# A fifth sequence unit in seven block products, a new order of the first tiles, shifted due times in the planner, and vector sums moved in the last quarter

## The chip, the cores and the metric

The kernel runs on one core of a Trainium2 chip. The metric is the device time of one execution in microseconds (us). Five engines work in parallel, each through its own instructions in its own order: TensorE (PE in the profile; its weight loads are listed as PEld), VectorE (DVE), ScalarE (ACT), GpSimd (POOL) and SyncE (SP), which here only issues DMAs. An instruction waits until what it reads has been written, and until what it overwrites has been read.

## The reference

Two sublayers on 2048 rows of 448 values, in fp32:

```
h  = x + Re(DFT_seq(DFT_hid(layernorm(x))))
     a = xn @ Wd_re^T ; b = xn @ Wd_im^T
     y = Ws_re @ a - Ws_im @ b
h2 = h + (gelu(hn @ w_gate) * (hn @ w_up)) @ w_down      with hn = layernorm(h)
```

w_gate and w_up are 448x1792, w_down is 1792x448. The two sequence matrices are 2048x2048.

## The kernel before

**Precision.** Every fp32 operand is split into two f16 parts, a high one (`hi_part`, a copy on ScalarE, line 105) and a low one, the remainder (`lo_part`, on VectorE, lines 109 and 111). Each product takes three matmuls (high by high, low by high, high by low).

**Stage 1, both transforms.** x stands in 16 tiles of 128 rows. A slot `F i` makes the hidden transform of tile i: 22 matmuls of 448 columns (`feature_mm`, line 456) into two PSUM banks. Two tiles make a unit u (0 to 7). The sequence transform runs in 8 passes p; each pass makes 256 output rows, and in it a slot `U p u` multiplies one unit's features with one block of the sequence matrix (`seq_mm`, line 573). There are two forms of it. A plain unit takes 24 matmuls of 448 columns. An S unit writes the 2x2 block product as seven products (Strassen's scheme): 42 matmuls of 224 columns. It needs sums of the blocks on both sides: of the features, once (`feature_sums`, `sums_high`, `sums_low`, lines 493 to 505), and of the weights, in each pass (`seq_sums`, lines 517 to 521, then `seq_high_s` and `seq_low_s` into the tile `wss`). Before, units 4 to 7 are S units and 0 to 3 are plain (`S_UNITS`, `is_s`). The `F` slots are mixed with the slots of pass 0. Rings: `wr` (raw weights by DMA) has 3 buffers, `ws` (their split) 4, `wss` 2, `wsum` 1.

In the same stretch VectorE and ScalarE also prepare gate and up weights for stage 2 (`Weights`, tiles `gu_s` and `gu_p`), mix finished passes into h (`seq_out`), and take its norm.

**The order in stage 1.** The first three slots (F0, F1, F2) and what they need are written out by hand, from the first load to the last `feature_mm(2, ...)`. Everything after is ordered by a planner: `Task` objects with an engine, a cost, a due time and predecessors. `arranged()` steps through model time; whenever an engine is free it gives it the able task with the earliest due time. The result is only an order of instructions for each engine; on the chip they run when their inputs are there. The slots themselves have a fixed order.

**Stage 2, gate, up, down.** A loop of 56 steps t (four quarters q of 14). In each step PE makes three accumulations X, Y, Z (`GateUp`, matmuls in line 1187), and from t = 14 on the 21 matmuls of one chunk of the down product (`dn_mm`, line 1132). In a step with q of 1 or more, each engine gets its part of this in this order:

- `prev.c_last`: ScalarE's gelu of `c`, then GpSimd's product `hh` (lines 1262, 1264)
- `x_close`; `z_open`, which writes bank Z again and so waits until the step before has read it (`c`, below)
- `dn_split(d+1)`: the next chunk's split, two copies on ScalarE and two low parts on VectorE (line 109)
- 8 matmuls of `dn_mm`; `y_mid`: matmuls into Y, a copy `u` on ScalarE, and on VectorE `hh <- Z, u` (line 1197), which reads Z
- `dn_ahead`: sums for a later chunk, two on GpSimd, one on VectorE (lines 1278 to 1280)
- `do(t, 6)`: in the last quarter the same three sums, all on VectorE, for chunks of the last two row blocks: in t = 44, 46, ... 54, and in 45 and 51
- 10 matmuls of `dn_mm`; `x_open` of the next step
- `y_close` (VectorE reads Y, line 1254); `z_close`: matmuls into Z, which wait until `hh <- Z, u` has read it, then VectorE's `c <- Z, u` (line 1197)
- the last 3 matmuls of `dn_mm`, `y_open`, and `do(t, 7)`: in the step after each of the extra sums their split, `dn_split`, again two copies on ScalarE and two low parts on VectorE.

Of the kernel before, what the change touches and what calls it, by code (L numbers as in the profile page):

```python
# [1 line left out]

# [11 lines left out]
P = 128  # L14
# [18 lines left out]
def kernel(  # L33
# [287 lines left out]
    S_UNITS, WR_BUFS, WS_BUFS, WSS_BUFS, STAGE_BUFS = (4, 5, 6, 7), 3, 4, 2, 2  # L321
# [146 lines left out]
    def is_s(u):  # L468
        return u in S_UNITS
# [30 lines left out]
    def sums_high(i):  # L500
        t = bop[i] = dft.tile([P, 2, 7, HD], F16, name=f"b{i}")
        hi_part(t[:, 0], b32[i][:, 1:8])

    def sums_low(i):
        lo_part(bop[i][:, 1], b32[i][:, 1:8], bop[i][:, 0])
# [57 lines left out]
    def seq_mm(p, u, first, last):  # L563
# [4 lines left out]
        for cc in range(2):  # L568
# [7 lines left out]
            if is_s(u):  # L576
# [132 lines left out]
    plain = [u for u in ORDER if not is_s(u)]  # L709
# [6 lines left out]
    for p in range(1, N_PASS):  # L716
        slots += [("U", p, u) for u in mixed if ("U", p, u) not in early]
# [12 lines left out]
    class Task:  # L730
        def __init__(self, engine, cost, due, what, after=(), begin=0.0, lag=0.15):
            self.engine, self.cost, self.due, self.what = engine, cost, due, what
            self.after, self.begin, self.lag = [t for t in after if t], begin, lag
            self.end = None

    FIRST = 3
    COST = {"F": 4.16, "P": 4.54, "S": 4.02}
    spans = [COST["F" if s[0] == "F" else "S" if is_s(s[2]) else "P"] for s in slots]
# [7 lines left out]
    def chain(engine, costs, due, make, after=()):  # L746

        run, last = [], list(after)

        def step(first):  # L750
            if first:
                run.append(make())
            next(run[0])

        for k, cost in enumerate(costs):
            last = [add(engine, cost, due, lambda k=k: step(k == 0), after=last)]
        return last[0]
# [4 lines left out]
    def fixed(n, rank, engine, cost, what, after=(), lag=0.0):  # L762
        if n < FIRST:
            plan(n, rank, what)
            return None
        return add(engine, cost, T[n + 1], what, after=after, begin=T[n] - 1.0, lag=lag)
# [3 lines left out]
    for k, (i, i2) in enumerate(tiles_of):  # L770
        n = where["F", i]
        if k > 2:
            t = fixed(n - 10, 8, "SP", 0.1, lambda u=i // 2: x_load(u), lag=5.0)
            t = fixed(n - 7, 7, "V", 1.35, lambda i=i, j=i2: x_stats(i, j), [t])
            t = fixed(n - 6, 2, "A", 0.3, lambda i=i, j=i2: x_root(i, j), [t])
            if n - 6 < FIRST:
                fixed(n - 6, 5, "V", 0.6, lambda i=i, j=i2: x_rstd(i, j))
            else:
                t = chain("V", (0.2, 0.1, 0.1, 0.1), T[n - 5], lambda i=i, j=i2: x_rstd_steps(i, j), [t])
            t = fixed(n - 6, 5, "V", 0.15, lambda i=i, j=i2: x_bias(i, j), [t])  # L780
        for c in (i, i2):
            n = where["F", c]
            if k > 2:
                low = fixed(n - 5, 5, "A", 1.15, lambda i=c: x_norm(i), [t])
                low = fixed(n - 5, 5, "V", 0.85, lambda i=c: x_lo(i), [low])
            if k >= 2:
                turned[c] = fixed(n - 4, 2, "SP", 0.1, lambda i=c: x_turn(i), [low] if k > 2 else (), lag=5.0)
                steps[n].after += [t for t in [turned[c]] if t]
        for c in (i, i2):
            n = where["F", c]  # L790
            if not k:
                continue
            done = [steps[n]] if n in steps else []
            if is_s(c // 2):
                t = drained = add("A", 1.05, T[n + 1] + 1.5, lambda i=c: feature_high(i), after=done + ring_w[-2:][:1] * (len(ring_w) > 1))
                t = chain("V", (0.56, 0.36, 0.36), T[n + 2], lambda i=c: feature_sums(i, V), [t])
                t = add("A", 1.45, T[n + 2] + 2.0, lambda i=c: sums_high(i), after=[t])
                t = add("V", 1.7, T[n + 2] + 3.5, lambda i=c: sums_low(i), after=[t])
                ring_w.append(t)
            else:  # L800
                t = add("A", 0.95, T[n + 1] + 1.0, lambda i=c: feature_high(i), after=done)
                t = drained = add("V", 1.07, T[n + 1] + 2.5, lambda i=c: feature_low(i), after=[t])
            bop_of[c] = t
            out_of[n] = drained
    for n, s in enumerate(slots):
        if n < FIRST:
            continue
        if s[0] == "F":
            past = [m for m in out_of if m < n]
            steps[n].after += [out_of[m] for m in sorted(past)[:-1]]  # L810
        elif s[1] == 0:
            steps[n].after += [bop_of[c] for c in (2 * s[2], 2 * s[2] + 1) if c in bop_of]
# [3 lines left out]
    for g, (p, u) in enumerate(units):  # L816
# [5 lines left out]
        else:  # L822
            load = add("SP", 0.1, T[n] - 12.0, lambda p=p, u=u: seq_load(p, u), after=done_with[g - WR_BUFS], lag=5.5)
        if not g:
            done_with[g] = []
            continue
        room = [steps[where["U", *units[g - WS_BUFS]]]] if g >= WS_BUFS else []
        size = 0.9 if is_s(u) else 1.0
        high = add("A", size, T[n] - 1.6, lambda p=p, u=u: seq_high(p, u), after=[load] + room)
        low = add("V", 1.02 if is_s(u) else 1.16, T[n] - 0.4, lambda p=p, u=u: seq_low(p, u), after=[high])  # L830
        done_with[g] = [low]
        if is_s(u):
            t = chain("V", (0.6, 0.34, 0.34), T[n] - 3.0, lambda p=p, u=u: seq_sums(p, u), [load] + sums_of)
            room = [steps[s_units[-WSS_BUFS]]] if len(s_units) >= WSS_BUFS else []
            high_s = add("A", 0.98, T[n] - 1.5, lambda p=p, u=u: seq_high_s(p, u), after=[t, high] + room)
            low_s = add("V", 1.16, T[n] - 0.3, lambda p=p, u=u: seq_low_s(p, u), after=[high_s])
# [8 lines left out]
    for p in range(N_PASS):  # L845
# [3 lines left out]
        load = fixed(n - 6 if p < 2 else n0 - 5, 9, "SP", 0.1, lambda p=p: h_tile(p), h_done.get(p - 4, ()), lag=6.0)  # L849
        if p >= 2:  # L850
            seed = add("A", 1.0, T[n0] - 1.0, lambda p=p: seq_seed(p), after=[load] + rooms[p - 2], begin=T[n0 - 3])
# [4 lines left out]
        copy = add("A", 0.35, t0 + 1.0, lambda p=p: seq_copy(p), after=[steps[n - 1], load] + last_e)  # L856
        mixed_in = chain("V", (1.4 if p < 2 else 0.32, 0.64, 0.86, 0.56), t0 + 5.0, lambda p=p: seq_out(p), [copy])
        rooms[p] = [mixed_in]
        store = add("SP", 0.1, t0 + 6.0, lambda p=p: h_store(p), after=[mixed_in], lag=6.0)
        m = [add("A", 1.75, t0 + 9.0 + 4 * g, lambda q=q, j=j, g=g, p=p: ffn_moments(q, j, hp[q, j], g, junk_of(e_of[p])), after=[mixed_in]) for g in range(2)]  # L860
        t = add("A", 0.25, t0 + 14.0, lambda q=q, j=j: ffn_root(q, j), after=m)
        t = chain("V", (0.2, 0.1, 0.1, 0.1), t0 + 15.0, lambda q=q, j=j: ffn_rstd_steps(q, j), [t])
        last_e, h_done[p] = m, [store, t]
        if q < 2:
            t = add("V", 0.15, t0 + 16.0, lambda q=q, j=j: ffn_bias(q, j), after=[t])
            t = add("A", 1.35, t0 + 17.0, lambda q=q, j=j: ffn_norm_act(q, j, hp[q, j]), after=[t])
            h_done[p] = [store, t]
            for k in range(4):
                t = add("V", 0.36, t0 + 18.0 + k, lambda q=q, j=j, k=k: ffn_sums(q, j, (k,)), after=[t])
            for k in range(2):  # L870
                high = add("A", (0.65, 1.0)[k], t0 + 22.0 + k, lambda q=q, j=j, k=k: ffn_hi(q, j, (k,)), after=[t])
                t = high
            for k in range(5):
                t = add("V", (0.34, 0.87, 0.25, 0.35, 0.25)[k], t0 + 23.0 + k, lambda q=q, j=j, k=k: ffn_lo(q, j, (k,)), after=[t])
            last_e = [t]
            for k in range(4):
                add("SP", 0.1, t0 + 28.0 + k, lambda q=q, j=j, k=k: ffn_transpose(q, j, (k,)), after=[t])
# [17 lines left out]
    begin0 = 12.0  # L895
    raw, freed, stages = None, [], []
    for k, f in enumerate(order):
        gap = (at_end - 10.0 - begin0) / N_DFT
        t0 = begin0 + gap * k
        due = lambda part: t0 + gap * part  # L900
        s1 = add("V", 0.83, due(0.2), lambda f=f: gu[f].sums(True, False), after=[raw] + freed, begin=t0 - 10.0)
        s2 = add("V", 0.95, due(0.3), lambda f=f: gu[f].sums(False, True), after=[s1])
        t, lows = s2, []
        for m in range(4):
            room = stages[-STAGE_BUFS : len(stages) - STAGE_BUFS + 1]
            high = add("A", (0.55, 0.35, 0.55, 0.55)[m], due(0.35 + 0.2 * m), lambda f=f, m=m: gu[f].high(m), after=[t] + room)
            low = add("V", (0.6, 0.34, 0.6, 0.6)[m], due(0.4 + 0.2 * m), lambda f=f, m=m: gu[f].low(m), after=[high])
            stages.append(add("N", 0.0, 0.0, lambda: None, after=[low], lag=7.0))
# [3 lines left out]
        if k + 1 < N_DFT:  # L912
            raw = add("SP", 0.1, due(0.8), lambda f=order[k + 1]: gu_begin(f), after=lows[:2] + [s2], lag=6.5)

    for f in range(2):
        fixed(len(slots) - 6 + 2 * f, 9, "SP", 0.1, lambda f=f: gw_first(f))
    t = fixed(len(slots) - 14, 9, "SP", 0.1, lambda: down_load(0), last_e, lag=6.0)
# [685 lines left out]
```

## Time and profile before

| | us |
|---|---|
| median of 3 runs (712.10 to 712.65) | 712.17 |
| the profiled execution's own time | 712.42 |
| its span, first to last instruction | 710.6 |
| PE busy | 701.3 (99%) |
| DVE busy | 544.6 (77%) |
| ACT busy | 399.8 (56%) |
| POOL busy | 197.1 (28%) |

The granted clock of PE is 1.000 over the span. Times in the rows of the trace count from the first instruction; 1.8 us of the execution's own time lie outside the span. Stage 1 goes to 354.3 us on PE, stage 2 from there to the end. A busy PE is not a PE at its peak; what counts is where its idle time stands and how long a slot lasts.

### The profile page before, as it was taken

The numbers are of one execution on the slowest core, as the hardware profiler recorded it, in microseconds if no ns is written. First come the engines' busy times: TensorE is split into PE (matmuls) and PEld (weight loads), VectorE is DVE, ScalarE is ACT, GpSimd is POOL, SyncE is SP. The second block draws the span as 40 slices with busy tenths as digits, with TensorE's granted clock in tenths as the row PEclk, the third lists the DMA queues.
The fourth block names the chain that finished last, engine by engine and source line by source line (L and its number), as shares of the span: only waits on it lengthen the run. The fifth ranks groups of instructions, "written<-read, shape, count | busy, mean of one in ns | idle before, by whom it ended". The sixth has DMA issues, their size and how long they took to land.

```text
span 710.6 us, 15025 instructions
## 1 busy us (share of the span) xinstructions
PE 701.3 (99%) x5902; PEld 570.6 (80%) x5902; DVE 544.6 (77%) x1131; ACT 399.8 (56%) x845; POOL 197.1 (28%) x225
## 2 busy tenths in 40 slices
PE   7999999999999999999999999999999999999998
PEld 4556567777776868686888889999999999998898
DVE  6799999899988987877368667575765755887876
ACT  5587574757656665645166665555555544454432
POOL 0000000000000000002026664474664745656442
PEclk9999999999999999999999999999999999999999
DMA  9366846799988697758267745847468574445301
GB/s 330 102 151 177 209 155 200 250 206 328 245 221 284 191 245 252 258 162 318 92 238 300 271 172 171 187 165 201 176 196 188 178 208 162 176 156 178 134 28 53
DMA packets 82935, 140.64 MB, mean 198 GB/s; under 512 B 41776, under 2 KB 60464, under 8 KB 82864
## 3 DMA queue, kind: packets, MB, share of 16 engines
q1 hardware_dynamic: 82864, 139.68, 63.8%
q8 instruction: 46, 0.75, 0.4%
q14 instruction: 25, 0.20, 0.1%
HBM read 110.17 MB, written 20.19 MB: 183 GB/s over the span
## 4 chain that ended last, share of the span: by engine, by line
PE 92%; DVE 3%; ACT 2%; issue 1%; DMA 1%; SPq 0%; DVEq 0%; ACTq 0%
PE acc L573 39%; PE acc_d L1132 15%; PE pY L1187 13%; PE pZ L1187 9%; PE ab L456 9%; PE pX L1187 8%; DMA wh_raw<-in_w_hid_dram 1%; DVE dn_w L109 1%; ACT dn_w L105 1%; DVE wh_lo L111 0%; DVE hh L1197 0%; ACT c L1262 0%; DVE dn_s L1280 0%; DVE dn_s L1279 0%; ACT u L1231 0%
## 5 line engine op out<-in xcount | busy, mean ns | idle before, releaser
L1187 PEld LDWEIGHTS <-gw 128*128 128x128 f16 x2184 | 213.3, 98 | 25.4 <-issue 3.0
L573 PE MATMUL acc<-b,ws 128*128 128x448 f16 (+1 forms) x1344 | 221.9, 312 | 0.0
L573 PEld LDWEIGHTS <-ws 128*128 128x128 f16 x1344 | 130.6, 98 | 70.7
L1187 PE MATMUL pY<-hops,gw 128*128 128x256 f16 x952 | 129.1, 273 | 0.0
L1132 PE MATMUL acc_d<-wd,dn_w 128*128 128x224 f16 x1050 | 122.3, 259 | 0.0
L234 POOL TENSOR_TENSOR wd_s<-wd 128x448 f32<-128x448 f32 x7 | 8.4, 1207 | 350.2 <-DMA wr<-in_w_seq_dram 331.7
L1132 PEld LDWEIGHTS <-dn_w 128*128 128x128 f16 x1050 | 101.2, 98 | 2.8
L105 ACT ACTIVATE ws<-wr 128x256 f16<-128x256 f32 (+2 forms) x96 | 63.1, 693 | 61.4 <-PE acc L573 43.5
L573 PE MATMUL acc<-b,wss 128*128 128x224 f16 x768 | 94.5, 259 | 0.0
L1187 PE MATMUL pZ<-hops,gw 128*128 128x256 f16 x616 | 85.5, 272 | 1.9 <-DVE c L1197 1.4
L1264 POOL TENSOR_TENSOR hh<-hh,c 128x256 f32<-128x256 f32 x56 | 45.6, 815 | 145.4 <-ACT c L1262 144.9
L1187 PE MATMUL pX<-hops,gw 128*128 128x256 f16 x616 | 83.3, 273 | 0.0
L111 DVE SCALAR_TENSOR_TENSOR ws<-wr,ws 128x256 f16<-128x256 f32 (+2 forms) x96 | 72.3, 781 | 9.1 <-ACT ws L105 9.0
L573 PEld LDWEIGHTS <-wss 128*128 128x128 f16 x768 | 73.8, 98 | 0.0
L109 DVE TENSOR_TENSOR dn_w<-hh,dn_w 128x256 f16<-128x256 f32 x50 | 25.7, 515 | 50.3 <-ACT dn_w L105 50.0
L456 PEld LDWEIGHTS <-xT 128*128 128x128 f16 x352 | 34.2, 98 | 32.5 <-issue 1.4
L109 DVE TENSOR_TENSOR dn_w<-dn_s,dn_w 128x640 f16<-128x640 f32 x50 | 54.9, 1098 | 7.0 <-ACT dn_w L105 5.9
L1231 ACT ACTIVATE u<-pY 128x256 f32<-128x256 f32 x56 | 21.4, 383 | 61.7 <-PE pY L1187 61.7
L1279 POOL TENSOR_TENSOR dn_s<-hh 128x256 f32<-128x256 f32 x42 | 52.8, 1258 | 0.0
L1226 ACT ACTIVATE pY<-pX 128x256 f32<-128x256 f32 x56 | 20.6, 368 | 50.0 <-PE pX L1187 50.0
L111 DVE SCALAR_TENSOR_TENSOR wss<-wsum,wss 128x1024 f16<-128x1024 f32 x32 | 39.3, 1229 | 9.8 <-ACT wss L105 9.8
L456 PE MATMUL ab<-wh_hi,xT 128*128 128x448 f16 x224 | 45.6, 352 | 0.5 <-DVE wh_hi L435 0.2
(120 smaller groups left out, 906.5 us busy)
## 6 DMA issues: line engine op xcount, KB each, us to landing
gw<-w_dram SPq DMA_DIRECT2D x54, 896.0 KB, 4.9
wr<-in_w_seq_dram SPq DMA_DIRECT2D x64, 512.0 KB, 4.6
gu_raw<-in_w_gu_dram SPq DMA_DIRECT2D x28, 384.0 KB, 4.4
w_dram<-gu_p SPq DMA_DIRECT2D x36, 256.0 KB, 3.0
hx<-in_x_dram SPq DMA_DIRECT2D x8, 448.0 KB, 6.3
h_dram<-hx SPq DMA_DIRECT2D x8, 448.0 KB, 5.3
hr<-h_dram SPq DMA_DIRECT2D x8, 448.0 KB, 5.4
x<-in_x_dram SPq DMA_DIRECT2D x7, 448.0 KB, 6.2
```

Source lines behind the costliest of these rows:

```text
L105: A.activation(dst, src, AF.Copy, scale=scale)
L109: V.tensor_sub(dst, src, hi)
L111: V.scalar_tensor_tensor(dst, src, scale, hi, op0=ALU.mult, op1=ALU.subtract)
L234: G.tensor_sub(s[:, 2:4], t[:, 0:2], t[:, 2:4])
L456: PE.matmul(feat[i][r][:, :D], xT[i][:, kx, :], w[:, kw, r * D : (r + 1) * D], start=n == 0, stop=n == 10,)
L573: PE.matmul(banks[k][:, cols], lhs, rhs, start=k not in begun, stop=stop, skip_group_check=True)
L1132: PE.matmul(acc[k // 2][:, k % 2 * HD : (k % 2 + 1) * HD], a_of(la, a), b_of(lb, b), start=first and m == 0 and k % 2 == 0, stop=last and ...
L1187: PE.matmul(ps, w[:, wl, wa + ws, :], ops[:, m + ms, :], start=first and n == 0, stop=last and n == len(terms) - 1, skip_group_check=True,)
L1226: A.activation(self.Y, self.X, AF.Copy)
L1231: A.activation(self.u2, self.Y, AF.Copy, scale=SC)
L1264: G.tensor_mul(c22, c22, self.c12)
L1279: E.tensor_sub(s[:, 2:4], t[:, 1:4:2], t[:, 0:4:2])
```

## The change

1. Unit 3 becomes a mixed unit (`MIXED = 3, S_FROM = 5`): plain in passes 0 to 4, an S unit in passes 5, 6 and 7. Its two feature tiles get the sums, in tiles of 8 blocks in place of 4 (the other S units have 7). In the last three passes the order of the units is 0, 4, 1, 5, 3, 6, 2, 7, where it was 0, 1, 4, 2, 5, 3, 6, 7. The ring `ws` has 3 buffers in place of 4.
2. The hand-written beginning has another order: both statistics of tiles 2 and 3 together, matmuls of tile 1 ahead of the low parts of tile 0, and what belongs to tiles 10 and 11, to the drains of F0 to F2 and to the first weights goes to the planner.
3. The planner is driven by events, starts VectorE's tasks at -4.1, charges SP for its issues, can hold an engine for a task that is due earlier and able soon (`HOLD`), and adds a constant to the due time of each kind of task (`SHIFT`).
4. In stage 2 the extra vector sums of the last quarter move from `do(t, 6)` to a new `do(t, 8)` at the end of the step, behind `c` and behind `do(t, 7)`.

```diff
-    S_UNITS, WR_BUFS, WS_BUFS, WSS_BUFS, STAGE_BUFS = (4, 5, 6, 7), 3, 4, 2, 2
+    S_UNITS, WR_BUFS, WS_BUFS, WSS_BUFS, STAGE_BUFS, MIXED, S_FROM = (4, 5, 6, 7), 3, 3, 2, 2, 3, 5
...
-    def is_s(u):
-        return u in S_UNITS
+    def is_s(u, p=N_PASS):
+        return u in S_UNITS or u == MIXED and p >= S_FROM
...
     def sums_high(i):
-        t = bop[i] = dft.tile([P, 2, 7, HD], F16, name=f"b{i}")
-        hi_part(t[:, 0], b32[i][:, 1:8])
+        k0 = i // 2 != MIXED
+        t = bop[i] = dft.tile([P, 2, 8 - k0, HD], F16, name=f"b{i}")
+        hi_part(t[:, 0], b32[i][:, k0:8])
...
-            if is_s(u):
+            if is_s(u, p):
                 for a, o, k, half in PRODUCTS:
+                    o += u == MIXED
...
     for p in range(1, N_PASS):
+        if p == S_FROM:
+            mixed = [0, 4, 1, 5, 3, 6, 2, 7]
         slots += [("U", p, u) for u in mixed if ("U", p, u) not in early]
...
-        def __init__(self, engine, cost, due, what, after=(), begin=0.0, lag=0.15):
-            self.engine, self.cost, self.due, self.what = engine, cost, due, what
+        def __init__(self, engine, cost, due, what, after=(), begin=-4.0, lag=0.15, kind=None):
+            self.engine, self.cost, self.due, self.what = engine, cost, due + SHIFT.get(kind, 0.0), what
...
+    SHIFT = {"copy": 40.9, "fhigh": -85.4, "fhighp": -21.3, "flow": -2.3, "fsum": 12.6, "guhi": 34.6, "gulo":
...
+    HOLD = (0.52, 5.1)
...
-    begin0 = 12.0
+    begin0 = 22.2
...
-        gap = (at_end - 10.0 - begin0) / N_DFT
+        gap = (at_end - 5.3 - begin0) / N_DFT
...
     def arranged():
...
+        free = {"V": -4.1, "A": -0.9, "G": 0.0, "N": -9.0, "SP": -9.0, "PE": 0.0}
...
+            t = able[e][0][2]
+            soon = [w[2].at for w in waiting[e] if e in "VA" and w[0] < now + HOLD[0] * t.cost and w[2].due + HOLD[1] < t.due]
+            if soon:
+                free[e] = min(soon)
+                continue
...
     x_turn_pe(0, 0, 4)
+    x_rstd(1)
     wh_high(1, V)
     x_turn_pe(0, 4, 7)
-    x_rstd(1)
-    wh_high(2)
     x_norm_v(1)
     x_high(1)
-    wh_high(3)
+    wh_high(2)
     feature_mm(0, range(4))
     x_lo(1)
+    x_turn_pe(1, 0, 3)
+    wh_high(3)
+    x_stats(2, 3)
+    x_root(2, 3)
+    feature_mm(0, range(4, 6))
+    x_turn_pe(1, 3, 7)
     wh_low(0)
-    feature_mm(0, range(4, 6))
...
-    feature_mm(0, range(6, 8))
-    x_rstd(2)
+    feature_mm(0, range(6, 7))
+    x_rstd(2, 3)
     x_norm(2)
-    feature_mm(1, range(4))
+    feature_mm(1, range(7))
     wh_low(1)
     x_lo(2)
...
-        at(side, (t, 6), lambda n=n: dn_sums(6 * NC + n, V))
+        at(side, (t, 8), lambda n=n: dn_sums(6 * NC + n, V))
         at(side, (t + 1, 7), lambda n=n: dn_split(6 * NC + n, spare(n, 6 * NC + n) if n < 4 else None))
     for n, t in enumerate((3 * NF + 3, 3 * NF + 9)):
-        at(side, (t, 6), lambda n=n: dn_sums(7 * NC + n, V))
+        at(side, (t, 8), lambda n=n: dn_sums(7 * NC + n, V))
         at(side, (t + 1, 7), lambda n=n: dn_split(7 * NC + n, spare(4 + n, 7 * NC + n)))
...
             dn_ahead(t)
-            do(t, 6)
             dn_mm(d, range(8, 18))
...
             do(t, 3)
             do(t, 7)
+            do(t, 8)
```

Here `FIRST` is 3, `NF` is 14 and `NC` is 7. The split of each extra sum stays at `do(t + 1, 7)`.

More of the change, by code (lines that the diff above doesn't have):

```diff
@@ L1 @@
 from contextlib import ExitStack
+from heapq import heappop, heappush
 import concourse.bass as bass
@@ L708 @@
         ready.append(u)
-    plain = [u for u in ORDER if not is_s(u)]
+    plain = [u for u in ORDER if not is_s(u, 0)]
     late = [("U", 0, v) for v in sorted(ready, key=lambda v: ORDER.index(v))]
@@ L744, in add, with chain @@
         return tasks[-1]
-    def chain(engine, costs, due, make, after=()):
+    def chain(engine, costs, due, make, after=(), kind=None):
         run, last = [], list(after)
@@ L755, in chain @@
         for k, cost in enumerate(costs):
-            last = [add(engine, cost, due, lambda k=k: step(k == 0), after=last)]
+            last = [add(engine, cost, due, lambda k=k: step(k == 0), after=last, kind=kind)]
         return last[0]
@@ L781 @@
         for c in (i, i2):
             n = where["F", c]
[L783 to L793, printed above, removed]
+            done = [steps[n]] if n in steps else [add("N", 0.0, 0.0, lambda: None, begin=(-1.8, -1.0, 0.1)[n])]
@@ new lines, in arranged @@
+        free = {"V": -4.1, "A": -0.9, "G": 0.0, "N": -9.0, "SP": -9.0, "PE": 0.0}
+        last = None
+        for n in range(FIRST, len(slots)):
+            steps[n].after = [a for a in steps[n].after if a] + ([last] if last else [])
+            last = steps[n]
+        left, next_of, begun = {}, {}, []
+        waiting = {e: [] for e in free}
+        able = {e: [] for e in free}
+        everything = tasks + [steps[n] for n in range(FIRST, len(slots))]
+        number = {id(t): k for k, t in enumerate(everything)}
@@ new lines, in arranged @@
+        for t in everything:
+            t.at = t.begin
+            left[id(t)] = len(t.after)
+            for a in t.after:
+                next_of.setdefault(id(a), []).append(t)
+            if not t.after:
+                heappush(waiting[t.engine], (t.at, number[id(t)], t))
+        while len(begun) < len(everything):
+            best = None
+            for e in free:
+                at = free[e] if able[e] else max(free[e], waiting[e][0][0]) if waiting[e] else None
+                if at is not None and (best is None or at < best[0]):
+                    best = at, e
+            now, e = best
+            while waiting[e] and waiting[e][0][0] <= now:
+                _, k, t = heappop(waiting[e])
+                heappush(able[e], (t.due, k, t))
+            t = able[e][0][2]
[3 more added lines that the diff above has]
+                continue
+            heappop(able[e])
+            cost = t.cost
+            if e == "V" and free["G"] > now:
+                cost += min(free["G"] - now, 1.9 * cost) * 0.9 / 1.9
+            t.start, t.end = now, now + cost
+            free[e] = t.end
+            begun.append(t)
+            for n in next_of.get(id(t), ()):
+                lag = 0.0 if t.engine == "PE" and n.engine == "PE" else t.lag
+                n.at = max(n.at, t.end + lag)
+                left[id(n)] -= 1
+                if not left[id(n)]:
+                    heappush(waiting[n.engine], (n.at, number[id(n)], n))
@@ L952, in arranged @@
+        begun.sort(key=lambda t: t.start)
+        number = {id(steps[n]): n for n in steps}
+        begun = [(t.start, number.get(id(t), t)) for t in begun]
         return begun
```

197 lines of the change are left out of this document (83 added, 114 removed).

## The prediction

> **What bounds the kernel now.** I read the busy time by stretch first, then what PE waited for.
>
> ```profile
> PE 701.3 (99%) x5902; PEld 570.6 (80%) x5902; DVE 544.6 (77%) x1131; ACT 399.8 (56%) x845; POOL 197.1 (28%) x225
> ```
>
> ```profile
> 37.00:125.00 88.00, 88.00 (x565) 54.67 (x564) 84.35 (x176) 59.15 (x97) 0.00 (x0) 1.00 0.64 180
> 251.00:354.00 103.00, 103.00 (x799) 77.03 (x798) 73.21 (x137) 50.58 (x98) 4.01 (x3) 1.00 0.70 223
> 7.72:24.66 16.94, 14.84 (x87) 7.58 (x88) 14.46 (x45) 8.46 (x17) 0.00 (x0) 1.00 0.63 237
> 24.66:354.00 329.34, 329.34 (x2410) 232.97 (x2409) 279.62 (x577) 201.03 (x365) 4.01 (x3) 1.00 0.74 218
> ```
>
> The columns are the stretch, its length, then PE, PEld, DVE, ACT and POOL busy. From 24.66 us, where F3 starts, to 354 PE never rests. So in stage 1 time is won only by cheaper matmuls or by an earlier F3, ahead of which PE idles 16.94 - 14.84 = 2.1 us. DVE has little room in the feature part (84.35 of 88) and more in the last three passes (73.21 of 103). In stage 2 PE waits on DVE here:
>
> ```profile
> PE pZ L1187 <- DVE c L1197: 1.4, 2, 0.7
> ...
> PE pZ L1187 <- DVE hh L1197: 0.3, 1, 0.3
> ```
>
> ```profile
> 648.77 0.82 PE L1187 MATMUL pZ<-hops,gw 128*128 128x256 f16 x6 [0.68 <-DVE c L1197]
> 662.26 0.82 PE L1187 MATMUL pZ<-hops,gw 128*128 128x256 f16 x6 [0.68 <-DVE c L1197]
> ```
>
> Both waits of 0.68 are `z_open`, in steps t = 51 and 53. The row of `hh` shows that `z_close` waits in the same way for `hh <- Z, u`. What DVE is late beyond the slack of these two reads, PE loses.
>
> **The change part by part: the fifth unit.** One plain and one S slot, in the chain of waits:
>
> ```profile
> 41.85 4.54 PE acc L573 x24
> ...
> 63.04 4.03 PE acc L573 x42
> ```
>
> Three slots change form: 3 x (4.54 - 4.03) = 1.53 us less.
>
> [...]
>
> What it adds on DVE, by groups:
>
> ```profile
> L111 DVE SCALAR_TENSOR_TENSOR wss<-wsum,wss 128x1024 f16<-128x1024 f32 x32 | 39.3, 1229 | 9.8 <-ACT wss L105 9.8
> ...
> L517 DVE TENSOR_TENSOR wsum<-wr 128x512 f32<-128x512 f32 x32 | 21.9, 686 | 6.1 <-DMA wr<-in_w_seq_dram 5.9
> ...
> L109 DVE TENSOR_TENSOR b<-b,b 128x1568 f16<-128x1568 f32 x8 | 14.3, 1789 | 0.6 <-ACT b L105 0.3
> ...
> L521 DVE TENSOR_TENSOR wsum<-wsum,wr 128x256 f32<-128x256 f32 x32 | 13.4, 420 | 0.2
> ...
> L111 DVE SCALAR_TENSOR_TENSOR b<-ab,b 128x448 f16<-128x448 f32 x16 | 9.2, 616 | 1.5 <-ACT b L105 1.5
> ...
> L493 DVE TENSOR_TENSOR b<-b 128x448 f32<-128x448 f32 x8 | 5.0, 621 | 0.6 <-ACT b L105 0.6
> ...
> L495 DVE TENSOR_TENSOR b<-b 128x224 f32<-128x224 f32 x8 | 3.1, 387 | 0.0
> ```
>
> Per pass 0.69 + 2 x 0.42 for the sums and 1.23 for their low part: 2.8, in three passes 8.3, against 103 - 73.2 = 29.8 idle there. The two feature tiles each add 0.62 + 2 x 0.39 + 1.79 x 8/7 - 2 x 0.62 = 2.2: 4.4, against 3.65 idle in the feature part. That fits only because the planner may delay preparing gate and up weights, whose sums and low parts stand there too:
>
> ```profile
> 25.00:125.00 100.00, 11.57 (x22) 1.00 0.64 178
> ```
>
> That is DVE on the tile of their sums, 11.57 us in 100; later there is room for it, up to the end of stage 1, where DVE idles 10.30 us on end:
>
> ```profile
> 353.12 0.39 DVE L611 SCALAR_TENSOR_TENSOR e<-acc,e 128x224 f32<-128x224 f32 x1 [10.30 <-PE acc L573]
> ```
>
> I cost the whole DVE side at nothing. Without that cover PE is late by the 4.4 - 3.65 = 0.8 that doesn't fit. The ring `ws` with 3 buffers leaves a split two slots, 8 us, for about 2.5. More tightly, in the order 5, 3, 6 the `wss` buffer of unit 6 comes free with the end of unit 5, so its high part on ScalarE and the 1.23 of DVE have the one slot of unit 3, 4.03. A missed slot costs at most that 1.23 per pass, 3.7 in all; no gain is possible, PE being full. I take 0, as in the other S slots of the trace. The DMAs stay the same in number and size; SP's queue only gets another order, and the wr loads keep their ring of 3.
>
> **The beginning.** The new order keeps every operation, so I followed it with the old durations.
>
> ```profile
> x<-in_x_dram SPq DMA_DIRECT2D x1, 448.0 KB, 7.7
> ```
>
> ```profile
> 3.55 0.97 SPq L338 DMA_DIRECT2D x<-in_x_dram  x2
> ...
> 18.94 1.08 DVE L111 SCALAR_TENSOR_TENSOR wh_lo<-wh_raw,wh_hi 64x896 f16<-64x896 f32 x1
> ...
> 20.55 1.14 DVE L353 BATCH_NORM_STATS2 st_x<-x 128x6 f32<-128x448 f32 x2
> ...
> 24.66 2.81 PE L456 MATMUL ab<-wh_hi,xT 128*128 128x448 f16 x14
> ```
>
> Tiles 2 and 3 land at 3.55 + 7.7 = 11.25. Their statistics now stand ahead of the first low part on DVE, which waits a microsecond for them, and their root stands on ScalarE ahead of the copy of tile 1's second half, for which PE waits some 0.5. Against that, 14 matmuls of tile 1 no longer wait behind tile 2. By this hand count PE idles 2.0 us where the same count of the old order gives 2.8; the last low part ends at 19.95 (20.02 before), and F3 starts at 24.05: 0.6 earlier. Ends: all 2.1 of the idle time gone, or 0.5 later if each engine's new neighbour is as late as that copy. What the planner now orders just behind (tiles 10 and 11, the drains of F0 to F2) is hidden by PE's F3 and first plain slot and taken as 0; uncovered, PE would pay its lateness whole.
>
> **The sums of the last quarter.** Moving them behind `c` removes both waits of `z_open`: -1.36. But in t = 45 and 51 `do(t, 7)` holds a split whose low parts wait on ScalarE, and the sums now queue behind it; the next split and `hh <- Z, u` queue behind the sums. DVE at t = 45 and 46, before:
>
> ```profile
> 613.22 0.88 DVE L1278 TENSOR_TENSOR dn_s<-hh 128x256 f32<-128x256 f32 x1
> ...
> 615.01 0.41 DVE L1254 SCALAR_TENSOR_TENSOR hh<-pY,g 128x256 f32<-128x256 f32 x1
> 615.35 0.41 DVE L1197 SCALAR_TENSOR_TENSOR c<-pZ,u 128x256 f32<-128x256 f32 x1
> 616.51 0.43 DVE L109 TENSOR_TENSOR dn_spare<-hh,dn_spare 128x256 f16<-128x256 f32 x1 [0.75 <-ACT dn_spare L105]
> 617.13 0.83 DVE L109 TENSOR_TENSOR dn_spare<-dn_s,dn_spare 128x640 f16<-128x640 f32 x1 [0.20 <-ACT dn_spare L105]
> 618.02 0.81 DVE L109 TENSOR_TENSOR dn_w<-hh,dn_w 128x256 f16<-128x256 f32 x1
> 618.75 1.34 DVE L109 TENSOR_TENSOR dn_w<-dn_s,dn_w 128x640 f16<-128x640 f32 x1
> 620.02 0.41 DVE L1197 SCALAR_TENSOR_TENSOR hh<-pZ,u 128x256 f32<-128x256 f32 x1
> ...
> 620.76 0.41 DVE L1278 TENSOR_TENSOR dn_s<-hh 128x256 f32<-128x256 f32 x1
> ...
> 621.63 0.41 DVE L1254 SCALAR_TENSOR_TENSOR hh<-pY,g 128x256 f32<-128x256 f32 x1
> ```
>
> ```profile
> 619.82 0.71 PE L1187 MATMUL pY<-hops,gw 128*128 128x256 f16 x5
> 620.48 0.71 PE L1187 MATMUL pZ<-hops,gw 128*128 128x256 f16 x5
> ```
>
> ```profile
> 617.48 1.07 POOL L1264 TENSOR_TENSOR hh<-hh,c 128x256 f32<-128x256 f32 x1 [2.88 <-ACT c L1262]
> ...
> 619.38 1.31 POOL L1279 TENSOR_TENSOR dn_s<-hh 128x256 f32<-128x256 f32 x1
> ```
>
> `hh` at 620.02 lets `z_close` start at 620.48: the read has no slack left even before. The three sums take 615.01 - 613.22 = 1.79 beside POOL and 621.63 - 620.76 = 0.87 without it. Put at 618.0, they run beside POOL, busy 617.48 to 620.69, and end at 619.8; the first low part follows to 620.5, the second, mostly past POOL, takes about 0.9, `hh` starts at 621.4 and `z_close` at 621.9: 1.4 late. In t = 46 the split of 45's sums again precedes that step's own sums, so t = 47 repeats it, and 51 does the same to 52 and 53: 4 x 1.4 = 5.6. Ends: 0.87 each (3.5) if nothing is slowed, 1.79 each (7.2) if POOL slows all. The steps with sums alone (44, 48, 50, 54) have DVE idle behind `c`: 0. Net 5.6 - 1.36 = +4.2, between +2.1 and +5.8.
>
> [...] The trace has 0.88 against 0.41 for the first of these sums, a slowing and no full block, and I go by it.
>
> **Sum.** -1.53 - 0.6 + 4.2 = +2.1 on the profiled execution's 712.42, or 714.5; that execution lies 0.25 above the median of 712.17, so 714.3.
>
> **Rivals.** (a) *The sums find room*: ScalarE's copies come so early that DVE does the extra split in its 0.75 of idle time, and only the two waits of 0.68 go: -1.36 - 1.53 - 0.6 = -3.5, 708.7. It decides if `hh` starts before 619.9 in t = 46. Against it: 620.02 without the sums in front. (b) *Unslowed sums*: 3.5 - 1.36 - 2.1 = 0, 712.2. For it: POOL's work is the same and only its overlap shifts. (c) *Unit 6 starves*: part of the 3.7 above, say 2, on top: 716.3. For it: three S slots in a row, which no pass had; against it 29.8 us of idle DVE. (d) *The change doesn't do what it says*: DVE's load in the feature part swallows the gain of the fifth unit and F3's: 716.4.
>
> **How the numbers follow.** A measurement of this kernel can tell about 0.2%, 1.4 us, from no change. Chances: my forecast 0.45, (a) 0.28, (b) 0.17, (c) 0.06, (d) 0.04. The forecast's own range, with stalls from 1.1 each to the upper end of 1.79, is 713.1 to 715.8 (a lower price is rival b); about a seventh of its 0.45 lies under 713.6. Faster than 710.75: (a), 0.28. Slower than 713.6: the rest of the forecast, (c) and (d), 0.48. Between: that seventh and (b), 0.24. The range reaches down to (a), where 708.4 leaves out 0.12, and up to 716.5.
>
> **What would show it.** Right: PE `pZ` rows with 1.3 to 1.8 idle released by `hh` in t = 46, 47, 52, 53, no `z_open` released by `c`, the vector sums right before the next split's low parts, F3 near 24.05, S slots of 4.03 for unit 3, PE full to about 352. Wrong: no wait on `hh` above 0.5 in that quarter, or PE gaps ahead of unit 6 in passes 5 to 7.

## The result, and the profile after

| | before | after |
|---|---|---|
| median, us | 712.19 (712.10 to 712.65, 4 runs) | 716.20 (715.20 to 717.14, 4 runs) |
| the profiled execution's own time, us | 712.42 | 716.53 |
| its span, us | 710.6 | 714.8 |
| granted clock of the profiled execution | 1.000 | 0.998 |

The other timed runs of after had a clock of 0.997 or 0.998 too. The ratio is 1.0055, with a 95% interval of 1.0041 to 1.0069: the changed kernel is slower by 0.55%. The profiled execution is 4.1 us longer. Three cuts through the trace, each at an instruction that both kernels have, tell where.

First the timeline of PE in the changed kernel, with three of its instructions: F3, the slot F10, and the first accumulation of stage 2. Columns are start, duration, engine and line, operation, count, and in brackets the idle time before it and what ended it.

```profile
24.83 2.81 PE L457 MATMUL ab<-wh_hi,xT 128*128 128x448 f16 x14
...
33.76 2.82 PE L457 MATMUL ab<-wh_hi,xT 128*128 128x448 f16 x14
...
351.70 0.82 PE L1202 MATMUL pX<-hops,gw 128*128 128x256 f16 x6
```

The same view of the kernel before:

```profile
33.37 2.81 PE L456 MATMUL ab<-wh_hi,xT 128*128 128x448 f16 x14
...
352.85 0.82 PE L1187 MATMUL pX<-hops,gw 128*128 128x256 f16 x6
```

- Up to F3: 24.83 against 24.66, so +0.17.
- F3 to F10: 8.93 against 8.71, so +0.22.
- F10 to stage 2: 317.94 against 319.48, so -1.54.
- Stage 2, from its first accumulation to the end of the span: 714.8 - 351.70 = 363.1 against 710.6 - 352.85 = 357.75, so +5.35.

The sum is +4.2, the difference of the spans. Stage 1 as a whole became 1.15 shorter, and stage 2 lost more than four times that. What PE waited for in the changed kernel (in all, times, longest) shows by what:

```profile
PE pZ L1202 <- DVE hh L1212: 6.9, 6, 2.3
...
PE xT_ps L419 <- DVE xs L110: 1.3, 2, 1.0
```

Before, the waits of `pZ` were 1.4 for `c` and 0.3 for `hh`, 1.7 together. Now none is for `c`, and those for `hh` make 6.9: +5.2 of the +5.35. In the timeline of PE after, the four large ones:

```profile
620.92 0.70 PE L1202 MATMUL pZ<-hops,gw 128*128 128x256 f16 x5 [1.35 <-DVE hh L1212]
...
628.70 0.71 PE L1202 MATMUL pZ<-hops,gw 128*128 128x256 f16 x5 [1.35 <-DVE hh L1212]
...
662.70 0.70 PE L1202 MATMUL pZ<-hops,gw 128*128 128x256 f16 x5 [2.27 <-DVE hh L1212]
...
670.48 0.71 PE L1202 MATMUL pZ<-hops,gw 128*128 128x256 f16 x5 [1.35 <-DVE hh L1212]
```

They are `z_close` of t = 46, 47, 52 and 53. The timeline of DVE after shows the queue that leads to the first:

```profile
615.54 0.43 DVE L110 TENSOR_TENSOR dn_spare<-hh,dn_spare 128x256 f16<-128x256 f32 x1 [1.24 <-ACT dn_spare L106]
616.17 0.83 DVE L110 TENSOR_TENSOR dn_spare<-dn_s,dn_spare 128x640 f16<-128x640 f32 x1 [0.20 <-ACT dn_spare L106]
616.91 0.95 DVE L1293 TENSOR_TENSOR dn_s<-hh 128x256 f32<-128x256 f32 x1
617.79 0.94 DVE L1294 TENSOR_TENSOR dn_s<-hh 128x256 f32<-128x256 f32 x1
618.65 0.81 DVE L1295 TENSOR_TENSOR dn_s<-hh 128x128 f32<-128x128 f32 x1
619.38 0.41 DVE L110 TENSOR_TENSOR dn_w<-hh,dn_w 128x256 f16<-128x256 f32 x1
619.72 0.81 DVE L110 TENSOR_TENSOR dn_w<-dn_s,dn_w 128x640 f16<-128x640 f32 x1
620.45 0.41 DVE L1212 SCALAR_TENSOR_TENSOR hh<-pZ,u 128x256 f32<-128x256 f32 x1
```

The first two rows are the extra split of t = 45, whose low parts wait for ScalarE's copies: DVE idles 1.24 and 0.20 us with three sums, ready to run, queued behind. Then the sums start, beside GpSimd, and take 619.38 - 616.91 = 2.47 us; the next split's low parts follow, then `hh <- Z, u` at 620.45, and PE's `z_close` starts 0.47 later.

The beginning shows something else. Windows of the changed kernel; columns are the stretch, its length, PE, PEld, DVE, ACT and POOL busy, the granted clock, the DMA share and GB/s:

```profile
7.00:8.20 1.20, 0.17 (x1) 0.10 (x1) 1.15 (x4) 0.29 (x1) 0.00 (x0) 1.00 0.94 335
8.20:9.69 1.49, 0.95 (x7) 0.38 (x7) 1.42 (x8) 1.07 (x2) 0.00 (x0) 1.00 1.00 384
9.69:13.10 3.41, 3.41 (x12) 1.63 (x12) 2.55 (x8) 2.21 (x4) 0.00 (x0) 0.52 1.04 404
13.10:16.00 2.90, 2.90 (x19) 1.62 (x18) 2.79 (x8) 1.89 (x4) 0.00 (x0) 0.97 1.05 391
```

PE was busy for 1.12 of the 2.69 us up to 9.69, and then the granted clock stood near one half for 3.41 us: 12 matmuls (transposes counted) where the 2.90 us behind hold 19. At the head of this stands a DVE instruction that came late, the statistics of tile 1:

```profile
7.02 0.63 DVE L354 BATCH_NORM_STATS2 st_x<-x 128x6 f32<-128x448 f32 x1 [1.04 <-DMA x<-in_x_dram]
```

Its tile landed late. Tile 1's load in the DMA issues of after, and then of before (the last column is us from issue to landing):

```profile
x<-in_x_dram SPq DMA_DIRECT2D x1, 224.0 KB, 5.3
```

```profile
x<-in_x_dram SPq DMA_DIRECT2D x1, 224.0 KB, 3.7
```

Over the nine profiled executions of the experiments below this load took 3.8 to 5.2 us. The one with 5.2 (the first experiment with the old first tiles) kept a clock of 1.00 all the same, so a late tile alone does not explain the half clock.

### The profile page after: what moved, and what is told of

The parts are those of the page before. It is cut to its first block, busy times and chain, and to the rows that moved or that the text cites. A ratio compares the mean times of both kernels' runs of the same rounds, so it can differ in the third digit from the quotient of the medians.

```text
span 714.8 us, 15160 instructions
## 1 busy us (share of the span) xinstructions
PE 701.5 (98%) x5956; PEld 577.1 (81%) x5956; DVE 555.3 (78%) x1145; ACT 405.5 (57%) x852; POOL 194.9 (27%) x225
## 4 chain that ended last, share of the span: by engine, by line
PE 90%; DVE 4%; ACT 3%; issue 1%; DMA 1%; SPq 0%; DVEq 0%; ACTq 0%
PE acc L576 37%; PE acc_d L1147 14%; PE pY L1202 13%; PE pZ L1202 9%; PE ab L457 9%; PE pX L1202 8%; DVE dn_w L110 1%; ACT dn_w L106 1%; DMA x<-in_x_dram 1%; DVE dn_s L1294 1%; DMA xT<-xs 0%; DVE dn_s L1295 0%; DVE hh L1212 0%; ACT b L106 0%; ACT ws L106 0%
## 5 line engine op out<-in xcount | busy, mean ns | idle before, releaser
L576 PE MATMUL acc<-b,ws 128*128 128x448 f16 (+1 forms) x1326 | 215.4, 308 | 0.0
L576 PEld LDWEIGHTS <-ws 128*128 128x128 f16 x1326 | 128.8, 98 | 64.1
L576 PE MATMUL acc<-b,wss 128*128 128x224 f16 x840 | 103.3, 259 | 0.0
L576 PEld LDWEIGHTS <-wss 128*128 128x128 f16 x840 | 80.8, 98 | 0.0
L110 DVE TENSOR_TENSOR dn_w<-dn_s,dn_w 128x640 f16<-128x640 f32 x50 | 53.2, 1065 | 7.2 <-ACT dn_w L106 6.1
L106 ACT ACTIVATE wss<-wsum 128x1024 f16<-128x1024 f32 x35 | 36.8, 1052 | 29.0 <-DVE wsum L524 22.3
L1294 POOL TENSOR_TENSOR dn_s<-hh 128x256 f32<-128x256 f32 x42 | 51.2, 1219 | 0.0
L112 DVE SCALAR_TENSOR_TENSOR wss<-wsum,wss 128x1024 f16<-128x1024 f32 x35 | 43.7, 1249 | 8.6 <-ACT wss L106 8.4
```

The costliest lines, as they stand in the source:

```text
L106: A.activation(dst, src, AF.Copy, scale=scale)
L110: V.tensor_sub(dst, src, hi)
L112: V.scalar_tensor_tensor(dst, src, scale, hi, op0=ALU.mult, op1=ALU.subtract)
L576: PE.matmul(banks[k][:, cols], lhs, rhs, start=k not in begun, stop=stop, skip_group_check=True)
L1294: E.tensor_sub(s[:, 2:4], t[:, 1:4:2], t[:, 0:4:2])
```

## The experiments

All times are medians. "After" is the changed kernel, 716.20, and "before" 712.19; the kernel before was timed again beside the experiments and gave 712.18, 712.39 and 712.27. No experiment leaves out a part of the computation.

**The order at the end of a step.** After, with the sums ahead of the split.

```diff
-            do(t, 7)
             do(t, 8)
+            do(t, 7)
```

> The changed kernel with the extra vector sums still behind c, but ahead of the split of that step instead of behind it. Theory (the sums queue behind a split that waits on ScalarE, and hh <- Z, u queues behind them): the sums run in the 0.75 to 1.3 us in which DVE waits for ScalarE, so the four waits of z_close (1.35, 1.35, 2.27, 1.35 = 6.3 us) go and the two waits of 0.68 at z_open do not come back; about 710 us. Rival (DVE simply has too much to do in steps 45 to 53, wherever the sums stand): at least two of the waits stay near 1.3 us, 713 us or more.

Measured: 709.57 (708.54 to 710.26, 4 runs), ratio to before 0.9962 [0.9948, 0.9976]. The windows of this kernel and then of the changed one, over the same stretch of the last quarter:

```profile
600.00:690.00 90.00, 90.00 (x870) 83.99 (x868) 68.58 (x135) 42.80 (x109) 47.83 (x53) 1.00 0.39 134
```

```profile
600.00:690.00 90.00, 83.67 (x800) 77.44 (x799) 64.55 (x123) 41.12 (x106) 45.18 (x53) 1.00 0.38 130
```

PE goes from 83.67 busy of 90 to 90.00. DVE's timeline in the experiment shows why:

```profile
613.27 0.42 DVE L1293 TENSOR_TENSOR dn_s<-hh 128x256 f32<-128x256 f32 x1
613.60 0.42 DVE L1294 TENSOR_TENSOR dn_s<-hh 128x256 f32<-128x256 f32 x1
613.94 0.28 DVE L1295 TENSOR_TENSOR dn_s<-hh 128x128 f32<-128x128 f32 x1
614.59 0.42 DVE L110 TENSOR_TENSOR dn_spare<-hh,dn_spare 128x256 f16<-128x256 f32 x1 [0.37 <-ACT dn_spare L106]
```

The sums fill the time in which DVE would wait for ScalarE's copy (0.37 of it is left), and there GpSimd is idle, so the first takes 0.42 and not 0.95. Swapping two calls changes the median by 716.20 - 709.57 = 6.6 us; the four waits themselves are 6.32. The profiled executions lie 7.6 apart, with part of it at the beginning, which the swap does not touch: here tile 1 landed after 3.9 us and F3 started at 23.38.

**The sums alone.** Before, with nothing changed but the place of the extra sums.

```diff
-        at(side, (t, 6), lambda n=n: dn_sums(6 * NC + n, V))
+        at(side, (t, 8), lambda n=n: dn_sums(6 * NC + n, V))
...
             do(t, 7)
+            do(t, 8)
```

> The kernel before with nothing changed but the place of the extra sums (end of the step, behind the split). Theory (the sums alone make the loss): the four waits of z_close come, 6.3 us, the two of 0.68 at z_open go; 712.2 + 6.3 - 1.4 = 717.1 us. Rival (they hurt only together with what the rest of the change shifts): 710.8 to 713 us.

Measured: 717.64 (716.88 to 718.30, 4 runs), ratio 1.0076 [1.0062, 1.0090]. What PE waited for:

```profile
PE pZ L1187 <- DVE hh L1197: 6.9, 6, 2.3
```

This is the wait of the changed kernel to the tenth. The move costs 5.4 us by itself and owes nothing to the rest of the change.

**The fifth unit taken out.** After, with `MIXED, S_FROM = -1, 99`.

```diff
-    S_UNITS, WR_BUFS, WS_BUFS, WSS_BUFS, STAGE_BUFS, MIXED, S_FROM = (4, 5, 6, 7), 3, 3, 2, 2, 3, 5
+    S_UNITS, WR_BUFS, WS_BUFS, WSS_BUFS, STAGE_BUFS, MIXED, S_FROM = (4, 5, 6, 7), 3, 3, 2, 2, -1, 99
```

> The changed kernel with unit 3 plain in all passes (and the old order of units in the last three). Theory (three slots at 4.54 against 4.03 us, all DVE work hidden): 1.5 us slower than the changed kernel, 717.7 us, stage 1 ending 1.5 us later. Rival (its DVE work cost as much elsewhere): within 0.5 us of the changed kernel's 716.2.

Measured: 721.33 (720.85 to 723.39, 4 runs), ratio 1.0126 [1.0111, 1.0142], 5.1 over after where 1.5 was expected. PE's timeline has new idle time in stage 1:

```profile
211.73 0.27 PE L576 MATMUL acc<-b,wss 128*128 128x224 f16 x1 [0.46 <-DVE wss L112]
...
240.60 6.59 PE L576 MATMUL acc<-b,ws 128*128 128x448 f16 x28 [3.22 <-DVE ws L112]
```

0.46 + 3.22 = 3.7, and with the 1.5 that makes 5.2. That this is near the 5.1 is in part chance: the profiled execution is 6.9 over after, with two stretches of 3.41 us at half clock (from 241.43 and from 668.10) and an F3 that starts 1.83 earlier. The planner made another order for this list of slots: DVE waits 2.08 us for a `wr` that SP issued only at 231.86, behind three transposing DMAs, and the low part for which PE waits stands behind that on DVE. So the run doesn't isolate the fifth unit. It suggests that the planner's new constants fit one list of slots.

**The fifth unit alone.** Before, with the fifth unit, its order of units and `ws` of 3 buffers, but the old planner, the old first tiles and the old place of the sums.

```diff
-    S_UNITS, WR_BUFS, WS_BUFS, WSS_BUFS, STAGE_BUFS = (4, 5, 6, 7), 3, 4, 2, 2
+    S_UNITS, WR_BUFS, WS_BUFS, WSS_BUFS, STAGE_BUFS, MIXED, S_FROM = (4, 5, 6, 7), 3, 3, 2, 2, 3, 5
...
+        if p == S_FROM:
+            mixed = [0, 4, 1, 5, 3, 6, 2, 7]
```

> The kernel before with the fifth unit alone (its feature sums, its seven products in passes 5 to 7, the new order of units there, ws with 3 buffers), ordered by the old planner with the old first tiles and the old place of the sums. Theory 1 (three slots 0.51 us shorter, DVE's part hidden by any planner that knows its costs): 712.2 - 1.5 = 710.7 us, PE without a wait in stage 1. Theory 2 (the new due times are needed: DVE in the feature part has 3.65 us idle for 4.4 more, and ws one buffer less): PE waits in stage 1 and the time is 711.5 us or more.

Measured: 717.25 (715.65 to 718.65, 6 runs), ratio 1.0065 [1.0050, 1.0080]. What PE waited for in stage 1, and three of these waits in its timeline:

```profile
PE acc L575 <- DVE wss L111: 3.0, 4, 1.1
PE acc L575 <- ACT wss L105: 2.3, 2, 1.2
```

```profile
116.08 0.36 PE L575 MATMUL acc<-b,wss 128*128 128x224 f16 x2 [1.22 <-ACT wss L105]
...
278.18 0.37 PE L575 MATMUL acc<-b,wss 128*128 128x224 f16 x2 [1.05 <-ACT wss L105]
279.63 0.27 PE L575 MATMUL acc<-b,wss 128*128 128x224 f16 x1 [1.08 <-DVE wss L111]
```

5.3 us of new waits, more than the 1.5 that the products save; behind the first of the three, from 117.34 on, the clock is also at half for 3.41 us. Four of them (3.2 together, up to 149 us) come at and behind the end of the stretch in which the features are prepared; the two at 278 and 279 (2.1) are unit 6 in the first of the last three passes, the third S slot in a row. In the changed kernel neither is there: over the last three passes its window has PE full, and unit 3's slots take 4.02 to 4.03 us.

```profile
251.00:352.00 101.00, 101.00 (x848) 81.49 (x846) 86.25 (x163) 54.37 (x106) 4.81 (x3) 1.00 0.72 228
```

DVE is fuller there than before (86.25 busy of 101, against 73.21 of 103), and hides it all. The new first tiles are not what removes the waits: the first experiment with the old first tiles (below) has the fifth unit and the new planner, and no wait of PE for `wss` among its waits. So the fifth unit paid only together with the new planner; which part of the planner does it (due times, `HOLD`, the events) was not separated.

**The first tiles.** Two runs with the old hand-written order of tiles 0 to 3: after with it, and the first experiment with it. What the old order had for tiles 10 and 11 there stays with the planner.

```diff
     feature_mm(0, range(4))
     x_lo(1)
-    x_turn_pe(1, 0, 3)
-    wh_high(3)
-    x_stats(2, 3)
-    x_root(2, 3)
     wh_low(0)
     feature_mm(0, range(4, 6))
+    x_turn_pe(1, 0, 4)
+    x_turn_pe(1, 4, 7)
+    x_stats(2)
...
-    feature_mm(1, range(7))
+    feature_mm(1, range(4))
```

> The changed kernel with the first tiles in the old order by hand up to the statistics of tiles 10 and 11, which stay with the new planner. Theory 1 (the new order itself leaves PE idle ahead of 9.7 us, so that the clock is halved for 3.4 us): clock back to 1.000 in all runs, F3 near 24.7 or earlier, 1 to 1.7 us faster than the changed kernel, 714.5 to 715.2. [...]

> The kernel of e1 (sums ahead of the split) with the first tiles in the old order, so that no wait of stage 2 hides what the beginning does. Theory 1 (the new order is worth what the profile of e1 shows, F3 at 23.38 against 24.66 us, and it alone brings the lower clock of some runs, 0.998, which cost 1.4 us there): F3 near 24.7, clock 1.000 in all runs, 709.9 to 710.2 us, against 708.5 to 709.0 for the runs of e1 at clock 1.000. Theory 2 (the early F3 is lost again behind it, at tiles 10 and 11): 708.6 to 709.2 us.

Measured: 716.78 (716.15 to 717.69, 5 runs), ratio 1.0066 [1.0053, 1.0078], and 709.28 (708.68 to 710.12, 5 runs), ratio 0.9956 [0.9945, 0.9968]. In the first, theory 1 fails (716.78, and 0.997 in two of five runs). But it does not decide on the beginning, since another place brought the low clock in its profiled execution, behind the 2.27 us of step 52:

```profile
663.00:666.50 3.50, 3.41 (x20) 2.60 (x20) 1.14 (x5) 0.87 (x3) 0.00 (x0) 0.60 0.78 250
```

The same stretch of the changed kernel, behind a wait just as long:

```profile
663.00:666.50 3.50, 3.50 (x36) 3.24 (x35) 1.80 (x5) 2.11 (x7) 0.41 (x1) 1.00 0.80 240
```

20 matmuls against 36. The second meets neither number: it ends level with the first experiment (709.28 against 709.57, intervals overlapping), so as it stands the new order of the first tiles gains nothing that the medians can tell. The two profiled executions, both at a clock of 1.000, do differ: F3 starts at 24.96 with the old order and at 23.38 with the new, and stage 2 at 351.60 and 350.76, so that about half of the early F3 is left there. Two of the four runs with the new order had the lower clock (0.998), and none of the five with the old was under 0.999.

**PE kept busy at the beginning.** The first experiment, with 16 transposes of the identity into a PSUM tile that nobody reads, put where PE idles in its first 14 us.

```diff
+    def idle_turns(n):
+        for k in range(n):
+            PE.transpose(pk[:, k % 8, :], ident, ident)
...
+    pk = ps_dft.tile([P, 8, P], F16, tag="A", name="pk")
+    idle_turns(3)
     x_rstd(1)
     wh_high(1, V)
     x_turn_pe(0, 4, 7)
+    idle_turns(1)
...
-    feature_mm(0, range(4))
+    feature_mm(0, range(1))
+    idle_turns(3)
+    feature_mm(0, range(1, 4))
     x_lo(1)
     x_turn_pe(1, 0, 3)
+    idle_turns(4)
...
-    feature_mm(1, range(7))
+    feature_mm(1, range(2))
+    idle_turns(5)
+    feature_mm(1, range(2, 7))
```

> The kernel of e1 with 16 transposes of the identity, whose result nobody reads, put into PE's idle places of the first 14 us (1.5 us of work where 1.7 us are idle). Theory 1 (the clock of 0.998 in two of four runs of e1 comes from a PE too idle there): clock 1.000 in nearly all runs, median 708.6 to 709.2, the spread under 1 us. Theory 2 (it comes from elsewhere, or from a late landing that some transposes can't bridge): clock 0.998 in about half of the runs as before, median 709.5 or more.

Measured: 708.12 (707.93 to 708.59, 5 runs), ratio to before 0.9941 [0.9928, 0.9954]. The window up to its F3, and F3 itself:

```profile
7.00:23.00 16.00, 15.60 (x108) 8.61 (x105) 13.66 (x38) 9.27 (x19) 0.00 (x0) 1.00 0.87 325
```

```profile
23.00 2.81 PE L457 MATMUL ab<-wh_hi,xT 128*128 128x448 f16 x14
```

PE has 15.60 of 16 busy, F3 starts 1.66 earlier than before, and the granted clock is 0.999 to 1.000 in all five runs. The early F3 is due to the order and not to the transposes: the run without the fifth unit has the same order, no transposes, and F3 at 23.00 too. The runs of the first experiment had either 1.000 (708.54 and 708.96) or 0.998 (710.17 and 710.26), about 1.5 us apart. Four runs against five are few; with after and the next two experiments, runs with this order had 0.998 or less in 6 of 8 without the transposes and in 1 of 20 with them. This is the fastest kernel of the study, 0.6% faster than before.

**The same in the changed kernel**, its sums left behind the split:

> The changed kernel (sums behind the split, all four waits) with the 16 transposes of e6 in the beginning. Theory 1 (the changed kernel lost its early F3 to a late landing and the halved clock): e6's 708.1 plus the four waits of 1.35, 1.35, 2.27, 1.35 us, 714.4 us, 1.5 to 2 us under the changed kernel, and the lower clock only in runs where a long wait of stage 2 brings it. Theory 2 (the waits of stage 2 bring the lower clock in most runs): 715.5 us or more, clock 0.998 in most runs.

Measured: 715.15 (714.58 to 716.15, 5 runs), ratio 1.0044 [1.0030, 1.0058]. F3 starts at 23.56, the four waits are 1.36, 1.36, 2.28 and 1.35. The beginning is worth 716.20 - 715.15 = 1.05 here, of the 1.8 expected; one of the five runs still had 0.997, and step 52 still had its long wait.

**Step 52.** The last experiment, with the drain's last two sums on GpSimd (line 1138) in step 51 and no longer in 52.

```diff
-            at(side, (t0 + 1 + n, 3), lambda p=p, n=n: drains[p].sums((2 * n, 2 * n + 1)))
+            at(side, (t0 + 1 + (min(n, 2) if p == 4 else n), 3), lambda p=p, n=n: drains[p].sums((2 * n, 2 * n + 1)))
```

> The kernel of e8 with the two last GpSimd sums of row block 4's drain made in step 51 and not in step 52. Theory 1 (the wait in step 52 is 2.27 and not 1.35 us because GpSimd's drain slows the two low parts ahead of hh <- Z, u): that wait falls to about 1.35 us, 0.9 us under e8, and the lower clock gets rarer. Theory 2 (step 52 is longer for what lies ahead of it): the wait stays above 2 us and the time within 0.3 us of e8.

Measured: 713.97 (713.55 to 714.63, 10 runs), ratio 1.0023 [1.0014, 1.0032], and a clock of 1.000 in all ten. PE's wait in step 52:

```profile
660.08 0.70 PE L1214 MATMUL pZ<-hops,gw 128*128 128x256 f16 x5 [1.36 <-DVE hh L1224]
```

2.28 became 1.36. Of the 1.2 us gained, 0.9 is this wait. The rest is not the edit's: the profiled execution without it has one more wait, of 0.28 at 382 us, and starts stage 2 0.29 later (350.47 against 350.18).

## Why the prediction was right or wrong

**The sums: right in mechanism and place, under-sized in one step.** The term was +4.2 net. `z_open` no longer waits, `z_close` waits for `hh` in the four steps named, and the vector sums stand between the two splits. Three of the waits are 1.35 where 1.4 was forecast, which is in part luck: the parts of the 1.4 were off and cancelled. The sums took 2.47 beside GpSimd, not 1.79, and the low parts behind them were past GpSimd and took 0.41 and 0.81, not 0.7 and 0.9. In step 52 they did not cancel, since GpSimd also has the drain there. DVE's timeline after, then GpSimd's:

```profile
660.25 0.88 DVE L110 TENSOR_TENSOR dn_w<-hh,dn_w 128x256 f16<-128x256 f32 x1
661.04 1.27 DVE L110 TENSOR_TENSOR dn_w<-dn_s,dn_w 128x640 f16<-128x640 f32 x1
662.24 0.41 DVE L1212 SCALAR_TENSOR_TENSOR hh<-pZ,u 128x256 f32<-128x256 f32 x1
```

```profile
660.14 1.50 POOL L1138 TENSOR_TENSOR hr<-hr,v 128x224 f32<-128x224 f32 x2
```

The four waits come to 1.35 + 1.35 + 2.27 + 1.35 = 6.32, less 1.36: +4.96, inside the ends of +2.1 and +5.8, though step 52 by itself is over the 1.79 that was taken as the most a step can lose. The mis-sized step is "51 does the same to 52 and 53", which took one pair of steps for the other without reading what GpSimd has in each. The last experiment shows it: without the drain, step 52 waits 1.36.

**The fifth unit: right.** -1.53 forecast, -1.54 from F10 to stage 2, with slots of 4.02 to 4.03 for unit 3.

**The DVE side at nothing: right for the changed kernel, and not for the reason given.** The argument was room in total (29.8 us idle in the last three passes, late weights elsewhere). The fifth unit under the old planner has the same room and waits 5.3 us. Room in a stretch did not tell; the order did, and the trace of before could not show the new one.

**The beginning: wrong.** The term was -0.6 and it measured +0.17 in the profiled execution. The step that failed is that all was followed "with the old durations": landing times and the clock were taken as fixed. In the changed kernel tile 1 landed after 5.3 us and not 3.7, and held DVE up by 1.04; PE idled; and the clock of the following matmuls was half for 3.41 us, a row that before does not have. What the landing costs without the half clock can be told only roughly: with the old order a landing after 5.2 us left F3 at 24.96, against 24.12 to 24.83 in the four executions with 3.7 to 3.9. The hand count of the order itself was too cautious: in the five other profiled executions of the new order, all at full clock there (three of them with the transposes), F3 starts at 23.00 to 23.56 where 24.05 was forecast. What stands just behind was taken as 0 and is +0.22: F3 to F10 takes 8.83 to 8.97 in all six executions with the new first tiles and 8.70 to 8.71 in all five with the old, whichever planner ordered the rest.

**The sum.** +2.1 forecast, +4.1 measured in the profiled execution. Of the 2.0 between, 0.72 is the sums (step 52's 2.27 - 1.4 = 0.87, less 0.05 in each of the others), 0.77 the beginning, 0.2 the stretch from F3 to F10, and 0.3 the smaller waits of stage 2 (0.6 in place of 0.3). The median, 716.20, lies above the forecast's own range of 713.1 to 715.8. It is inside the whole range only because that was drawn up to 716.5 for (c) and (d), neither of which happened.

**The rivals.** (a), that the sums find room, is false for the order as changed. With two calls swapped they do find room, though not by (a)'s reason (ScalarE's copies come no earlier; the sums stand ahead of the wait for them); at full clock that kernel took 708.54 and 708.96, near the 708.7 of (a). (b) would have needed no slowing by GpSimd; the first sum took 0.95 beside it. (c), unit 6 starving, does not happen in the changed kernel, but it happens in its place and at about its price (2.1 us) under the old planner. (c) gave 716.3 and (d) 716.4, both nearer the time measured than the forecast, by causes that the trace excludes: unit 6 has no wait, and the gain of the fifth unit is there in full.

**What stays open.** The timed runs have no trace, so how often late data and how often the wait in step 52 brought their lower clock is not known. Which part of the planner's change lets the fifth unit pay was not tried. Why tile 1 landed late in some executions is open too.

## What to carry to other kernels

In an engine's queue, put work that is ready ahead of work that waits for another engine: the same three sums cost 5.4 us behind a waiting split and nothing ahead of it. When a read of the next stage has no slack, follow it step by step through each step that repeats it, with what every other engine has in that step, since a price from one step need not hold in the next. Judge a planned order by its own trace, not by the idle total of a stretch.

## What the runs showed of the hardware

**The clock fell behind stretches that were only partly idle.** In the changed kernel PE idled at most 1.05 us at a time in the 2.69 us up to 9.69 and was busy 1.12 of them, and then ran at about half clock for 3.41 us. In the profile of the old first tiles the same came after a single wait of 2.27 us, while the changed kernel kept a clock of 1.00 behind an equal wait in the same step. With the old first tiles the half clock begins at 663.71, 0.62 behind the end of the wait (660.82 to 663.09); in the changed kernel the wait is at 660.43 to 662.70, and 0.62 behind its end is 663.32. The 3.41 us ahead of these two points and the 3.41 us behind them, with the old first tiles, then in the changed kernel (PE busy is the second number, the clock the third from the end):

```profile
660.30:663.71 3.41, 1.14 (x11) 0.86 (x10) 3.27 (x6) 0.37 (x1) 1.72 (x3) 1.00 0.22 83
663.71:667.12 3.41, 3.41 (x19) 2.48 (x18) 0.99 (x3) 1.49 (x4) 0.00 (x0) 0.50 0.78 258
```

```profile
659.91:663.32 3.41, 1.14 (x11) 0.87 (x10) 3.27 (x6) 0.37 (x1) 1.73 (x3) 1.00 0.22 81
663.32:666.73 3.41, 3.41 (x35) 3.16 (x34) 1.85 (x4) 2.34 (x7) 0.64 (x1) 1.00 0.78 236
```

PE was busy 1.14 us ahead of both points, and the clock is 0.50 behind one and 1.00 behind the other. So neither the length of the wait nor the busy time ahead of that point tells the two apart; what does was not shown. In the 3.41 us ahead of the five half-clock stretches of these traces PE was busy 0.83 and 1.31 (without the fifth unit, ahead of 241.43 and 668.10), 1.14 (the old first tiles), 1.29 (the fifth unit alone, ahead of 117.34) and 1.83 us (the changed kernel, ahead of 9.86): it was idle throughout in none of them. The price of one stretch is not traced: by an estimate from the rows above, a clock of 0.50 for 3.41 us is 1.7 us of PE's work, and the runs of the first experiment with the lower clock took about 1.5 us longer (708.54 and 708.96 against 710.17 and 710.26). Sixteen unread transposes in PE's idle time went with a clock of 0.999 or above in 19 of 20 runs; in the kernel of the first experiment the spread of the runs went from 1.7 us to 0.7.

**A vector sum took more than twice as long beside GpSimd.** A vector sum of 128x256 took 0.41 to 0.42 alone and 0.94 to 0.95 beside GpSimd's operations of 0.90 to 1.06, and both engines went on finishing one operation in about 0.88 us. That is less than the two take in turn: a GpSimd operation of this shape took 0.72 with DVE idle (at 679.21), and 0.41 + 0.72 = 1.13. So they do not seem to have run one after the other, as far as GpSimd's rough spans can tell. GpSimd's timeline after, beside the sums of t = 45 shown above, has these starts.

```profile
616.52 1.06 POOL L1279 TENSOR_TENSOR hh<-hh,c 128x256 f32<-128x256 f32 x1 [3.06 <-ACT c L1277]
617.54 0.90 POOL L1293 TENSOR_TENSOR dn_s<-hh 128x256 f32<-128x256 f32 x1
618.41 0.90 POOL L1294 TENSOR_TENSOR dn_s<-hh 128x256 f32<-128x256 f32 x1
```
